# Six h buffers in a pool of their own, spread transfers and later turns in a fused attention and gated-unit kernel

## The chip, the cores and the metric

The kernel runs on one core of a Trainium2 chip. The core's engines work side by side and meet only at semaphores: TensorE (PE in the profile, its weight loads PEld), VectorE (DVE), ScalarE (ACT), GpSimd (POOL) and SyncE (SP), which here only issues transfers. The metric is the device time of one execution in microseconds (us), the median of several runs; lower is better. A profiled execution is one more run, with its own time.

## The reference

All of it is float32, with 2048 positions, 640 channels and 1536 hidden units.

```python
xn = layernorm(x)                                  # x: (1, 2048, 640)
q, k, v = split(xn @ wqkv)                         # 32 heads of 20 channels
idx = pos[:, None] - 2 * arange(8)[None, :]        # each position sees itself and 7 earlier ones, 2 apart
logits = where(idx >= 0, q . k[idx] * 20 ** -0.5, -1e9)
o = softmax(logits) . v[idx]
s = o @ wo
h = (xn @ w_gate) * (xn @ w_up)                    # no nonlinearity between
out = x + s * silu(h @ w_down)
```

## The kernel before

**Arithmetic.** A matmul of full precision is made of three: each operand is split into a high part (ScalarE copies it to the matmul's type, L109 and others) and a low part (the difference, on GpSimd or VectorE, L110 and others), and high x high, high x low and low x high are added up in one PSUM bank. The profile shows 4054 such matmuls. Gate and up, the output projection and the down projection also use seven products in place of eight for a two by two block (`group`, `pair_product`, `product`), which costs sums of operands on VectorE and GpSimd and adds of results.

**Stages, in TensorE's order.** (1) To about 45 us x is loaded, normalised and transposed into xT, four chunks of 512 columns, each with a high and a low part. (2) To about 274 us the queries, keys and values are made, unit by unit: a unit is a group of 4 or 6 heads (GROUPS) at even or odd positions (r), 12 in all. ScalarE copies each result to a staging buffer (L441), and every second tile is sent to memory, qkv_scr (L445). Between these, gate and up are made for the first hidden blocks. (3) To about 525 us gate and up of the other blocks: `group(f, c0, second)` makes hidden block f for two chunks. (4) The output projection, in pairs of tiles (`pair_product`, L1033, p from 0 to 4) and then single tiles. (5) From about 600 us the down projection, the gate and the result.

**Attention** runs beside stages 2 and 3 on VectorE and GpSimd. It is a generator, `attention()`: `advance(budget)`, called after each piece of TensorE work, lets it emit as many of its steps as the budget pays for. This fixes the program order; nothing is reordered later, and each engine works its instructions off in order. For unit n a round goes over j = 0, 2, 4, 6: two keys' products (L527), one term of the values of unit n-1 (L498, its addition on GpSimd, L504), the reduction to logits (L534), another term of the values. After the round come the store of unit n-1's result (`store_o`, L575) and the softmax. `ahead(n, parts)` issues the loads of a unit on SP's queue: part 0 is `load_kq` (queries L408, keys L414 and L416), part 1 the values (the same lines, in the other half of the kv buffer). It does so once for each unit and part, and only when the unit is in qkv_scr. There are two kv buffers and one q buffer; ScalarE copies the queries on to PSUM (L488).

**The buffers of h.** Tag "gh" holds 128x512 tiles in 5 buffers. Each group takes four: `hold(j)` copies a partial product out of PSUM (L1295) for j = 0, 2, 1 and 4 of its order 0, 5, 2, 1, 4, 3, 6. Three banks A, C and B carry the seven products, so the next product into a bank waits until the hold before it has read that bank. The sums of a group are gate_b (L1298), up_b (L1301), gate_a (L1308), up_a (L1311) and h_b (L1304); up_a and h_b go to `unfinished` and are emitted by `finish_piece` after the first product of the next group. `store_h` (L1284) sends the two results to h_scr, and only then are two of the buffers free.

**SP's queue** carries loads and stores in program order; an instruction that waits holds up all those behind it. Before the change `group` issues the weights of the next block (`load_wf`, L175, two buffers "wraw") ahead of its first product, so they stand before the two h stores of the group before. GpSimd makes sums of weights (L1272, `w_add`) and low parts (L110, `w_split`).

**Early sums.** `early_sums(0)` is a generator of eight GpSimd steps (L593). EARLY of them are emitted ahead of `scales(8)`, three more behind it, the rest behind `scales(12)`. `spread(8)` multiplies the scales (L340) amid `gate_up(0, 1)`.

**The end of stage 3.** `beside` holds what is emitted after a named product: (f0, 1, 4) is `sums_wo` (L936 to L939), (f0, 1, 5) and (f0, 1, 6) the splits of wo's blocks 0 and 1 on VectorE, (f1, 0, 0) `turn_pair(0)` and `load_pair(1)`, where f0 = 10 and f1 = 11 are the last hidden blocks. `turn_pair(p)` is two transposes (L710) and four differences (L982 to L985) on VectorE; `hi_pair` (L1008, ScalarE) and `lo_pair` (L1012, VectorE) split its parts; `pair_product` adds up results at L1039, L1042 and L1044.

Of the kernel before, what the change touches and what calls it, by code (L numbers as in the profile page):

```python
# [43 lines left out]
PAIRS = range(0, W, 2)  # L44
PACE = 1.0
VEC = 3
EARLY = 3
GROUP_RATE = 0.184


# [6 lines left out]
def kernel(  # L57
# [15 lines left out]

    sb = ctx.enter_context(tc.tile_pool(name="sb", bufs=1))
    ps = ctx.enter_context(tc.tile_pool(name="ps", bufs=2, space=PSUM))
    dr = ctx.enter_context(tc.tile_pool(name="dr", bufs=1, space=DRAM))
    ctx.enter_context(tc.manual_schedule())

# [1 line left out]

    def st(shape, tag, bufs, dt=F32):
        cnt[0] += 1
        return sb.tile(shape, dt, tag=tag, bufs=bufs, name=f"{tag}_{cnt[0]}")

    ring, turns = [], [0]

# [333 lines left out]
    def qkv(m, r, i, runs=ALL_RUNS, at=None, act=None, bank=("q", 3)):  # L420

        c = MC[m]
        p = pt([P, 3 * c], *bank)
        t0 = (i % TPC) * P
        for n, (a, b, k) in enumerate(runs):
            if n == at:
                act()
            nc.tensor.matmul(p, xT[(r * NE + i) // TPC][a][:, k, t0:t0 + P], wq[m][b][k], start=n == 0,  # L428
                             stop=n == len(runs) - 1, skip_group_check=act is not None)
        if m or r:  # L430
            if not staged:
                y = slot([P, 2, 2 * 3 * CMAX], F32)
                staged.extend([y[:, 0], y[:, 1], st([P, 2 * 3 * CMAX], "pk", 1)])
            if c > CMAX and not wide:
                wide.extend([slot([P, 6 * c], F32), st([P, 6 * c], "pk", 1)])
            if i % 2 == 0:
                now[0] = wide if c > CMAX else staged
                now[0].insert(0, now[0].pop())
            n = len(MADE[m])
            y = now[0][0][:, :6 * c].rearrange("p (n a i c) -> p n a i c", n=n, a=3, i=2)  # L440
            nc.scalar.activation(y[:, :, :, i % 2, :].rearrange("p n a c -> p a n c"),  # L441
                                 p.rearrange("p (a n c) -> p a n c", a=3, n=n), AF.Copy)
            for k, g in enumerate(MADE[m]):
                if i % 2:
                    nc.scalar.dma_start(scr[2 * g + r][:, :, i - 1:i + 1, :], y[:, k])  # L445
                if i == NE - 1:
                    made.add(2 * g + r)
            if c > CMAX and (r, i) == (DIL - 1, NE - 1):
                staged.clear()
            return  # L450
        u = 0
        nc.scalar.activation(kv_t[u][:, :, W - 1 + i, :], p[:, c:].rearrange("p (a c) -> p a c", a=2), AF.Copy)
        nc.scalar.activation(q_t[u][:, i, :], p[:, :c], AF.Copy)
        for i0, i1 in ((1, 5), (5, NE)):
            if i == i1 - 1:
                for p0, p1 in ((0, 112), (112, 127)):
                    nc.sync.dma_start(kv_t[u][p0 + 1:p1 + 1, :, i0 - 1:i1 - 1, :],
                                      kv_t[u][p0:p1, :, W - 1 + i0:W - 1 + i1, :])


    def attention():
# [45 lines left out]
        for n, u in enumerate(ORDER + [None]):  # L507
            if u is not None:
                late_unit = u not in made
                while u not in made:  # L510
                    yield None
                ahead(n, (0, 1))
                for _ in range(5 if late_unit else 0):
                    yield None
                g, r = UN[u]
                nh = GROUPS[g]
                c = nh * DH
                copy_q(n)
                q, kv = q_two[:, :NE * c].unsqueeze(1).to_broadcast([P, 2, NE * c]), kv_t[u]
                lg = st([P, NE * nh, W], "lg", 2)  # L520
                t = twice.rearrange("p a c -> p (a c)")[:, :2 * NE * c].rearrange("p (a c) -> p a c", a=2)
            for j in PAIRS:
                if u is not None:
                    ahead(n + 1, (0,))
                    k = flat(kv[:, 0, j:j + NE, :])
                    k = bass.AP(k.tensor, k.offset, [k.ap[0], [c, 2], k.ap[1]])
                    nc.vector.tensor_mul(t, q, k)  # L527
                    yield 2 * NE * c * 1.22e-3
                if before is not None:
                    cost, add = values(j)  # L530
                    add()
                    yield cost
                if u is not None:
                    nc.vector.tensor_reduce(out=lg[:, :, j:j + 2].rearrange("p n a -> p a n"),  # L534
                                            in_=t.rearrange("p a (n d) -> p a n d", d=DH), op=ALU.add, axis=AX.X)
                    yield 2 * NE * c * 1.2e-3
                if before is not None:
                    cost, add = values(j + 1)
                    add()
                    yield cost  # L540
            if u is None:
                store_o(before)
                ring[:] = three
                return
            ahead(n + 1, (0, 1))
            if before is not None:
                store_o(before)
            m0 = lg[0:1].rearrange("p (i h) w -> p i h w", h=nh)
# [688 lines left out]
    def two(f):  # L1237
        return F_TWO <= f < f1
# [48 lines left out]
    def group(f, c0=0, second=0):  # L1287
# [26 lines left out]
        if not second:  # L1314
            if not two(f - 1):
                w_split(f, "U")
            w_sum.pop(f, None)
            wf_raw.pop(f)
            if f < f1 and f + 1 not in wf_raw:
                load_wf(f + 1)  # L1320
        for n, j in enumerate((0, 5, 2, 1, 4, 3, 6)):
            y = b["ACACABA"[j]]
            runs = [(w_unit(f, H_IN[j], k)[i], x_in(W_IN[j], l, k, c0)) for i, l in ALL3 for k in range(2)]
# [15 lines left out]
                places[second, n](f)  # L1339
            if (f, second, n) in beside:  # L1340
                beside[f, second, n]()
            advance(PACE * len(runs) * (GROUP_RATE if two(f) else 0.184))

    places = {}
# [54 lines left out]
    for m, t in ((m, t) for m in range(1, len(MADE)) for t in range(DIL)):  # L1399
# [23 lines left out]
        elif (m, r) == (last, 1):  # L1423
            for k in range(2):
# [3 lines left out]
    w_sum.pop(2)  # L1428
    load_wf(3)
    beside.update({(f0, 0, 5): lambda: advance(1e9), (f0, 1, 0): lambda: begin_last(), (f0, 1, 1): lambda: load_pair(0),  # L1430
                   (f0, 1, 4): lambda: sums_wo(), (f0, 1, 5): lambda: split_wo(0, nc.vector),
                   (f0, 1, 6): lambda: split_wo(1, nc.vector)})

    def begin_last():
        advance(1e9)
# [19 lines left out]
    for f in range(2, f1):  # L1455
# [18 lines left out]
        if f == F_TWO:  # L1474
# [1 line left out]
        group(f, 2)  # L1476
        group(f, 0, 1)
    places.clear()
    beside.update({(f1, 0, 0): lambda: (turn_pair(0), load_pair(1)), (f1, 0, 4): lambda: (hi_pair(0, 0), lo_pair(0, 0)),
                   (f1, 0, 6): lambda: (hi_pair(0, 1), lo_pair(0, 1), load_e(3, 1, 3)), (f1, 0, 5): sum_w5,  # L1480
                   (f1, 0, 3): lambda: load_e(3, 0, 2)})
    group(f1)
# [19 lines left out]
    split_wo(3)  # L1502
    split_w5()
    g3 = gate(f1, 3)
    turn_pair(2)
    up(f1, 3, g3)
    finish_piece()
    begin_wd()
    begin_wd("B22")
    pair_k.append(st([P, 3, HALF], "o", 1))  # L1510
    wd_steps = [(k, part) for k in range(KH) for part in range(2)]

    to_split = []
# [18 lines left out]
    for p in range(SP // 2):  # L1532
# [32 lines left out]
        pair_product(p, 5)  # L1565
        if p == 0:
            load_pair(4)
        elif p == 1:
            turn_pair(3)
        elif p == 2:  # L1570
            load_o(SP, 3, st([P, 3, D], "t", 2))
            turn_pair(4)
        else:
            if p == 3:
                load_o(SP + 3, 3, st([P, 3, D], "t", 2))
            wd_sums()
# [98 lines left out]
```

## Time and profile before

| | us |
|---|---|
| median of 3 runs | 748.58 (748.15 to 749.75) |
| the profiled execution, its own time | 748.28 |
| its span, first to last instruction | 746.5 |
| granted TensorE clock in it | 1.000 |
| ScalarE busy | 302.5 |
| GpSimd busy | 462.6 |
| transfers, mean | 178 GB/s |

A row of waits gives the engine with its tile and line, what released it, and then us in total, times, and the longest in us. A row of the timeline gives start and length in us, engine, line, operation, out<-in, sizes, how many instructions are merged, and in brackets how long the engine sat idle before and what ended that. A row of stretches gives from:to, length, then busy us of PE, PEld, DVE, ACT and POOL with the number of instructions, the granted clock, the transfers' share and GB/s. A row of the page's groups gives line, engine, operation, out<-in, sizes and count, then busy us and mean ns of one, then idle us before them and what ended most of it. A row of transfers gives tiles, issuing engine, count, KB each, and the median us from issue to landing. Lines such as L896 are line numbers of the kernel.

### The profile page before, as it was taken

The numbers are of one execution on the slowest core, as the hardware profiler recorded it, in microseconds if no ns is written. First come the engines' busy times: TensorE is split into PE (matmuls) and PEld (weight loads), VectorE is DVE, ScalarE is ACT, GpSimd is POOL, SyncE is SP. The second block draws the span as 40 slices with busy tenths as digits, with TensorE's granted clock in tenths as the row PEclk, the third lists the DMA queues.
The fourth block names the chain that finished last, engine by engine and source line by source line (L and its number), as shares of the span: only waits on it lengthen the run. The fifth ranks groups of instructions, "written<-read, shape, count | busy, mean of one in ns | idle before, by whom it ended". The sixth has DMA issues, their size and how long they took to land. (4 is left out here: it accounts for less than half of the span.)

```text
span 746.5 us, 11102 instructions
## 1 busy us (share of the span) xinstructions
PE 735.4 (99%) x4054; PEld 669.0 (90%) x4054; DVE 612.2 (82%) x720; ACT 302.5 (41%) x577; POOL 462.6 (62%) x389
## 2 busy tenths in 40 slices
PE   8999999999999999999999999999999999999997
PEld 6989989988999998778887888887899999999997
DVE  7666998699697887998999999667998777777775
ACT  5658413323332332233223322335556564444442
POOL 6169929787688878888879989877559800000000
PEclk9999999999999999999999999999999999999999
DMA  9465672947446548856165424268567655555534
GB/s 316 170 202 200 236 224 87 299 157 239 127 152 197 190 128 232 274 161 207 55 159 149 115 82 110 72 178 204 167 177 212 228 220 191 191 191 191 191 106 141
DMA packets 103493, 132.98 MB, mean 178 GB/s; under 512 B 22696, under 2 KB 74404, under 8 KB 103438
## 3 DMA queue, kind: packets, MB, share of 16 engines
q1 hardware_dynamic: 84686, 112.77, 48.4%
q10 hardware_dynamic: 17600, 14.26, 5.9%
q0 software_dynamic: 1152, 5.24, 2.2%
q8 instruction: 32, 0.52, 0.3%
q14 instruction: 23, 0.19, 0.1%
HBM read 83.58 MB, written 47.81 MB: 176 GB/s over the span
## 5 line engine op out<-in xcount | busy, mean ns | idle before, releaser
L504 POOL TENSOR_TENSOR o<-o,t 128x960 f32<-128x960 f32 (+1 forms) x69 | 139.6, 2024 | 19.1 <-DVE t L498 17.6
L498 DVE TENSOR_TENSOR t<-e,kv 128x960 f32<-128x960 f32 (+1 forms) x96 | 99.4, 1037 | 24.8 <-POOL o L504 24.7
L527 DVE TENSOR_TENSOR t<-q,kv 128x1920 f32<-128x1920 f32 (+1 forms) x48 | 92.4, 1925 | 4.3 <-DMA kv<-qkv_scr 4.2
L534 DVE TENSOR_REDUCE lg<-t 128x96 f32<-128x1920 f32 (+1 forms) x48 | 92.3, 1922 | 0.2
L428 PE MATMUL q<-s,xc 128*128 128x360 f32 (+1 forms) x450 | 83.1, 334 | 0.6 <-DVE lg L266 0.5
L110 POOL TENSOR_TENSOR s<-wraw,s 128x384 fp32r<-128x384 f32 (+6 forms) x58 | 69.6, 1210 | 19.9 <-ACT s L109 19.9
L428 PEld LDWEIGHTS q<-s,xc 128*128 128x128 f32 x450 | 74.9, 188 | 4.8 <-DVE lg L266 0.8
L1295 ACT ACTIVATE gh<-g 128x512 f32<-128x512 f32 x54 | 32.2, 597 | 115.8 <-PE g L1328 97.8
L428 PE MATMUL u<-s,xc 128*128 128x360 f32 (+1 forms) x360 | 65.8, 334 | 0.0
L428 PEld LDWEIGHTS u<-s,xc 128*128 128x128 f32 x360 | 60.3, 188 | 2.3
L428 PE MATMUL g<-s,xc 128*128 128x360 f32 (+1 forms) x330 | 61.5, 337 | 0.0
L428 PEld LDWEIGHTS g<-s,xc 128*128 128x128 f32 x330 | 55.7, 188 | 2.6
L1328 PE MATMUL u<-xc,s 128*128 128x512 f32 x216 | 55.3, 391 | 0.9 <-ACT gh L1295 0.9
L896 PE MATMUL q<-xc,s 128*128 128x320 f32 x342 | 55.5, 309 | 0.0
L1328 PE MATMUL g<-s,s 128*128 128x512 f32 x216 | 55.0, 390 | 0.0
L896 PEld LDWEIGHTS q<-xc,s 128*128 128x128 f32 x342 | 51.5, 188 | 0.0
L1328 PEld LDWEIGHTS u<-xc,s 128*128 128x128 f32 x216 | 40.3, 188 | 10.5 <-ACT gh L1295 2.0
L1328 PEld LDWEIGHTS g<-s,s 128*128 128x128 f32 x216 | 40.5, 188 | 8.6 <-ACT gh L1295 0.2
L109 ACT ACTIVATE s<-wraw 128x384 fp32r<-128x384 f32 (+6 forms) x59 | 33.5, 587 | 29.5 <-PE g L1328 9.0
L504 POOL TENSOR_TENSOR o<-t 128x960 f32<-128x960 f32 (+1 forms) x12 | 24.4, 2032 | 31.8 <-DVE t L498 25.2
L1328 PE MATMUL g<-xc,s 128*128 128x512 f32 x168 | 41.5, 391 | 1.3 <-ACT gh L1295 1.3
L119 PE MATMUL g<-xc,s 128*128 128x512 f32 (+1 forms) x180 | 40.1, 373 | 0.0
(367 smaller groups left out, 1566.5 us busy)
## 6 DMA issues: line engine op xcount, KB each, us to landing
h_scr<-gh SPq DMA_DIRECT2D x48, 256.0 KB, 2.6
wraw<-in_wgu SPq DMA_DIRECT2D x11, 640.0 KB, 4.4
kv<-qkv_scr SPq DMA_DIRECT2D x14, 480.0 KB, 5.9
qkv_scr<-s ACTq DMA_DIRECT2D x18, 360.0 KB, 4.4
t<-h_scr SPq DMA_DIRECT2D x8, 768.0 KB, 7.1
kv<-qkv_scr SPq DMA_DIRECT2D x14, 367.5 KB, 6.6
s_scr<-gh SPq DMA_DIRECT2D x16, 320.0 KB, 4.2
gh<-s_scr SPq DMA_DIRECT2D x16, 320.0 KB, 3.5
```

The costliest lines, as they stand in the source:

```text
L109: nc.scalar.activation(hi, raw, AF.Copy)
L110: eng.tensor_sub(lo, raw, hi.bitcast(F32))
L119: nc.tensor.matmul(acc, a, b, start=first and n == 0, stop=last and n == len(runs) - 1)
L428: nc.tensor.matmul(p, xT[(r * NE + i) // TPC][a][:, k, t0:t0 + P], wq[m][b][k], start=n == 0, stop=n == len(runs) - 1, skip_group_check=ac ...
L498: nc.vector.tensor_mul(t.rearrange("p (n d) -> p n d", d=DH), e[:, :, w].unsqueeze(2).to_broadcast([P, NE * nh, DH]), v)
L504: return NE * c * cost, lambda: eng.tensor_add(y, z, t)
L527: nc.vector.tensor_mul(t, q, k)
L534: nc.vector.tensor_reduce(out=lg[:, :, j:j + 2].rearrange("p n a -> p a n"), in_=t.rearrange("p a (n d) -> p a n d", d=DH), op=ALU.add, ax ...
L896: nc.tensor.matmul(p, y[:, i, k], wd_t[name][k][:, l], start=new and r == 0, stop=r == len(runs) - 1, skip_group_check=True)
L1295: nc.scalar.activation(kept[j], b["ACACABA"[j]], AF.Copy)
L1328: nc.tensor.matmul(y, w, x, start=j in (0, 1, 5) and r == 0, stop=r == len(runs) - 1, skip_group_check=True)
```

## The change

Six things, all in the order or the place of work; no matmul is added or removed.

- EARLY is 1 instead of 3.
- The tag "gh" moves out of the common pool into one of its own with 6 buffers, up to the last gate and up product. Then that pool is closed and one with 5 buffers takes its place.
- The four stores of staged results of unit 1 (m = 0, r = 1) are issued by SP instead of ScalarE.
- In attention the loads are spread: the values of unit n are asked for at j = 2 of its round (before: at the end of the round of n-1), the keys and queries of unit n+1 from j = 4 on (before: from j = 0 on). A unit that was made late still loads both at once.
- `group` issues the weights of the next block after its first product, so behind `finish_piece` and the two h stores.
- The splits of wo's blocks 0 and 1 each move by one product, `turn_pair(0)` and `load_pair(1)` by two, and `turn_pair(2)` from before the last up product to the end of pair 0, behind its sums and `load_pair(4)`.

```diff
-EARLY = 3
+EARLY = 1
...
+    halfway = ExitStack()
+    gh_pool = [halfway.enter_context(tc.tile_pool(name="six", bufs=1)), 6]
...
-        return sb.tile(shape, dt, tag=tag, bufs=bufs, name=f"{tag}_{cnt[0]}")
+        pool = sb
+        if tag == "gh":
+            pool, bufs = gh_pool
+        return pool.tile(shape, dt, tag=tag, bufs=bufs, name=f"{tag}_{cnt[0]}")
...
-                    nc.scalar.dma_start(scr[2 * g + r][:, :, i - 1:i + 1, :], y[:, k])
+                    (nc.scalar if m else nc.sync).dma_start(scr[2 * g + r][:, :, i - 1:i + 1, :], y[:, k])
...
-                ahead(n, (0, 1))
+                ahead(n, (0, 1) if late_unit else (0,))
...
-                    ahead(n + 1, (0,))
+                    if j == 2:
+                        ahead(n, (1,))
+                    elif j > 2:
+                        ahead(n + 1, (0,))
...
-            ahead(n + 1, (0, 1))
+            ahead(n + 1, (0,))
...
-            if f < f1 and f + 1 not in wf_raw:
-                load_wf(f + 1)
...
             if (f, second, n) in beside:
                 beside[f, second, n]()
+            if (second, n) == (0, 0) and f < f1 and f + 1 not in wf_raw:
+                load_wf(f + 1)
...
-                   (f0, 1, 4): lambda: sums_wo(), (f0, 1, 5): lambda: split_wo(0, nc.vector),
-                   (f0, 1, 6): lambda: split_wo(1, nc.vector)})
+                   (f0, 1, 4): lambda: sums_wo(), (f0, 1, 6): lambda: split_wo(0, nc.vector)})
...
-    beside.update({(f1, 0, 0): lambda: (turn_pair(0), load_pair(1)), (f1, 0, 4): lambda: (hi_pair(0, 0), lo_pair(0, 0)),
+    beside.update({(f1, 0, 0): lambda: split_wo(1, nc.vector),
+                   (f1, 0, 2): lambda: (turn_pair(0), load_pair(1)), (f1, 0, 4): lambda: (hi_pair(0, 0), lo_pair(0, 0)),
...
     g3 = gate(f1, 3)
-    turn_pair(2)
     up(f1, 3, g3)
...
     pair_k.append(st([P, 3, HALF], "o", 1))
+    halfway.close()
+    gh_pool[:] = [ctx.enter_context(tc.tile_pool(name="five", bufs=1)), 5]
...
         if p == 0:
             load_pair(4)
+            turn_pair(2)
```

## The prediction

> **What bounds the kernel now.** I read the page's shares first, then who TensorE waits for, then the stretches in which it waits.
>
> ```profile
> span 746.5 us, 11102 instructions
> ...
> PE 735.4 (99%) x4054; PEld 669.0 (90%) x4054; DVE 612.2 (82%) x720; ACT 302.5 (41%) x577; POOL 462.6 (62%) x389
> ```
>
> TensorE is busy 99% of the span and the change leaves its 4054 products alone, so it can win only what TensorE loses in waits. The waits of the matmuls, and below them those of the weight loads (us in total, times, longest):
>
> ```profile
> PE g L1328 <- ACT gh L1295: 1.3, 2, 0.9
> PE e L340 <- POOL lg L334: 1.0, 1, 1.0
> PE u L1328 <- ACT gh L1295: 0.9, 2, 0.6
> PE e L1033 <- DVE xc L1012: 0.8, 1, 0.8
> ...
> PEld g L1328 <- ACT gh L1295: 2.6, 4, 1.3
> PEld u L1328 <- ACT gh L1295: 2.0, 3, 1.0
> PEld e L340 <- POOL lg L334: 1.4, 1, 1.4
> ...
> PEld e L1033 <- DVE xc L1012: 1.0, 1, 1.0
> ...
> PEld g L1328 <- POOL pk L110: 0.5, 1, 0.5
> ```
>
> Three places carry nearly all of it: the gate and up products, which wait for ScalarE's copies into h buffers (L1295); the spread of the scales (L340), which waits for GpSimd; and the first output products (L1033), which wait for a low part on VectorE. (The last row, a wait for a split of weights, is touched by no edit.) A matmul's end is modelled, so its wait is the low bound of a loss; the weight load that stands before it waits longer and is the high bound. Low: 1.3 + 0.9 + 1.0 + 0.8 = 4.0 us. High: 2.6 + 2.0 + 1.4 + 1.0 = 7.0 us. More than 7.0 us isn't there to be won, while work moved to a worse place can cost more than that. How full the other engines are (busy us of PE, PEld, DVE, ACT, POOL in a stretch):
>
> ```profile
> 60.00:300.00 240.00, 240.00 (x1319) 223.75 (x1318) 198.74 (x182) 81.96 (x159) 190.87 (x139) 1.00 0.62 193
> 300.00:490.00 190.00, 188.27 (x824) 153.95 (x823) 174.17 (x170) 58.41 (x98) 161.85 (x122) 1.00 0.46 134
> ...
> 540.00:550.00 10.00, 10.00 (x70) 10.00 (x69) 9.81 (x18) 6.48 (x15) 5.51 (x5) 1.00 0.63 193
> ```
>
> Up to 300 us VectorE has 240 - 198.74 = 41 us to spare and GpSimd 49; beside the gate and up products 15.8 and 28.2; in the output products VectorE has 0.2 us in ten. These limits decide how much of a removed wait is kept.
>
> **EARLY from 3 to 1.** Two of GpSimd's early sums move behind scales(8).
>
> ```profile
> 43.79 2.55 POOL L593 TENSOR_TENSOR kv<-xc 128x512 f32<-128x512 f32 x2 [17.92 <-DVE xc L370]
> ...
> 45.02 0.17 DVE L277 RECIPROCAL lg<-lg 128x4 f32<-128x4 f32 x1
> ...
> 47.55 0.21 POOL L278 TENSOR_TENSOR lg<-lg 128x4 f32<-128x4 f32 x1
> ...
> 49.46 0.41 PE L340 MATMUL e<-lg,lg 128*128 128x32 f32 x2 [1.03 <-POOL lg L334]
> ```
>
> One sum (2.55 us for two) ends at 45.07, and the reciprocal that L278 needs ends at 45.19, so the scales start at 45.2 instead of 47.55. From there to the product it took 49.46 - 47.55 = 1.9 us: ready at 47.1, and TensorE asks at 49.46 - 1.03 = 48.4. The wait goes with 1.3 us to spare: 1.0 to 1.4, taken 1.2. The two sums come back behind scales(12), so GpSimd's early work ends about as much later as one of them lasts, 1.3 us; the 49 us that it has up to 300 hide that.
>
> **Stores of the first unit on SP's queue.** Four issues leave ScalarE. TensorE has no wait for L441's copies in the list, so nothing is won. On SP the last two stand behind the stores of early_high(1) and the copies into e_scr, and unit 1's keys are asked for behind them, so VectorE may start unit 1 later; its 41 us hide that, and without them the price is one wait for keys (4.2 us on VectorE, the row for L527 below). Taken 0 for TensorE, 0 to 4.2 if the cover is gone.
>
> **Six h buffers, and transfers spread.** What a copy into h waits for:
>
> ```profile
> 391.27 0.93 SPq L1284 DMA_DIRECT2D h_scr<-gh  x2
> ...
> 398.25 0.60 ACT L1295 ACTIVATE gh<-g 128x512 f32<-128x512 f32 x1 [2.98 <-DMA h_scr<-gh]
> ...
> 398.90 2.34 PE L1328 MATMUL g<-xc,s 128*128 128x512 f32 x9 [0.87 <-ACT gh L1295]
> ...
> 507.36 0.60 ACT L1295 ACTIVATE gh<-u 128x512 f32<-128x512 f32 x1 [2.63 <-POOL gh L1304]
> ```
>
> ```profile
> h_scr<-gh SPq DMA_DIRECT2D x48, 256.0 KB, 2.6
> ...
> kv<-qkv_scr SPq DMA_DIRECT2D x14, 480.0 KB, 5.9
> ```
>
> The two stores were out by 392.2, but the buffer came free only at 398.25, six us on, where the median store lands in 2.6: the next unit's queries and keys had been asked for just ahead of them. A group claims four buffers in 54 matmuls; at 2.34 / 9 = 0.26 us each that is 14 us, so a sixth buffer puts off each claim by up to 3.5 us. Of waits of 2.98 and 2.63 nothing is left then. Near 507 it helps further that both early splits of wo now stand behind the gate's sum on VectorE. The rows above give 2.2 to 4.6; taken 3.4. Where the five buffers follow the six, the first claim (L1039) may wait until the last h store has landed, 2.6 us at most, once; VectorE is ahead there by the move of turn_pair(2), so 0 is taken.
>
> The key loads that are asked for half a round later cost nothing by themselves:
>
> ```profile
> L527 DVE TENSOR_TENSOR t<-q,kv 128x1920 f32<-128x1920 f32 (+1 forms) x48 | 92.4, 1925 | 4.3 <-DMA kv<-qkv_scr 4.2
> ```
>
> After j = 4 two such products of 1.9 us are left, two reductions over the same elements, and the value products and softmax between them: 7.7 us and more, against 5.9 for a transfer. Without that cover VectorE waits, as it did once, for 4.2 us. Values have a whole round.
>
> The load of the next weights (load_wf) now stands behind both stores of the group before, and the second of them waits for GpSimd's L1304:
>
> ```profile
> 379.77 3.39 SPq L1284 DMA_DIRECT2D h_scr<-gh  x2
> ...
> 384.92 0.77 POOL L1272 TENSOR_TENSOR wraw<-wraw 128x256 f32<-128x256 f32 x1
> ...
> 421.63 1.57 POOL L110 TENSOR_TENSOR pk<-wraw,pk 128x640 fp32r<-128x640 f32 x1
> ...
> 425.65 1.52 PE L1328 MATMUL g<-xc,pk 128*128 128x512 f32 x6
> ```
>
> ```profile
> wraw<-in_wgu SPq DMA_DIRECT2D x11, 640.0 KB, 4.4
> ```
>
> In the tightest of seven groups it goes out at 379.77 + 3.39 = 383.2 and lands at 387.6, while the first sum over it began at 384.92: GpSimd waits 2.7 us, inside its 28.2. What matters more: weights for a next group were split by 423.20 and used at 425.65, 2.45 us on. With 1.2 + 3.4 = 4.6 us won, TensorE would come 2.1 us before them unless GpSimd and VectorE move up too, for which they have idle time in part. Given back: 0 to 2.1, taken 1.1.
>
> **Pairs turned later.** turn_pair(0) and the four transfers of load_pair(1) move by two products of a group; the wait of 3.79 us here takes that, since pair 0 is wanted only at 525.8:
>
> ```profile
> 519.33 0.69 DVE L1370 TENSOR_TENSOR gh<-g,gh 128x512 f32<-128x512 f32 x1 [3.79 <-PE g L119]
> ...
> 523.41 1.67 DVE L983 TENSOR_TENSOR t<-t,s 128x256 f32<-128x256 f32 x1
> ...
> 525.83 0.45 PE L1033 MATMUL q<-s,kv 128*128 128x320 f32 x2
> ```
>
> Pair 2 moves behind the sums of pair 0:
>
> ```profile
> 527.73 1.56 DVE L710 STREAM_TRANSPOSE s<-s 128x640 f32<-128x640 f32 x2
> ...
> 529.78 0.42 DVE L983 TENSOR_TENSOR s<-s,s 128x256 f32<-128x256 f32 x1
> ...
> 532.41 1.50 DVE L1012 TENSOR_TENSOR xc<-s,xc 128x640 fp32r<-128x640 f32 x1
> ...
> 533.96 0.56 PE L1033 MATMUL e<-s,xc 128*128 128x320 f32 x2 [0.78 <-DVE xc L1012]
> ...
> 541.13 0.48 DVE L1042 TENSOR_TENSOR gh<-o,e 128x320 f32<-128x320 f32 x1
> ...
> 543.12 1.04 PE L1033 MATMUL e<-xc,xc 128*128 128x320 f32 x6
> ```
>
> turn_pair(2) is 1.56 + 4 x 0.42 = 3.2 us, and the low part at 532.41 stands behind it. Without it that part is ready 3.2 us earlier and the wait is gone: 0.8 to 1.0, taken 0.9. The 3.2 us then fall before pair 1's sums. There L1042 ends at 541.61, and the product that overwrites its bank begins at 543.12: 1.5 us of room. The rest must fit into the time that VectorE no longer spends on it before. Given back: 0 to 3.2, taken 0.3, near the low end because the piece only changes places on an engine that was the late one here. Next late is L1042 in pairs 1 to 3.
>
> Four such differences took 1.67 us each beside GpSimd's splits (523.41) and 0.42 away from them (529.78). The Trainium skill (SBUF — State Buffer, Who interferes with whom) says that a VectorE tensor_tensor with both inputs in SBUF and a GpSimd instruction that reads SBUF shut each other out for a whole instruction; the trace agrees, 1.67 against 0.42, and by that rule the new place, next to the splits of wd, is the worse one. What such a place makes of the sum is rival 4.
>
> **Sum**, against the profiled execution's 748.28 us (0.3 below the median of the runs, 748.58): 748.28 - 1.2 - 3.4 - 0.9 + 1.1 + 0.3 = 744.2 us.
>
> **Rivals.** (1) Everything is kept, at the high bound: 748.28 - 7.0 = 741.3. For it: 15.8 and 28.2 us of idle time beside the groups; against: only 2.45 us of room before the weights. (2) Attention's two engines set the pace: the copies no longer wait, but the split weights come as late as before, and of the 3.4 us nothing is kept: 748.28 - 1.2 - 0.9 + 0.3 = 746.5. For it: VectorE is busy 174.17 of 190 us there. Against: only 0.5 us of weight loads waited for such a split. (3) The change doesn't do what it says: the copies wait for late work, not for a place, and new waits replace the old: about 748. (4) VectorE becomes the bound of the output products. It has 0.2 us in ten there, so turn_pair(2) is paid in full, and beside the splits of wd with 4 x (1.67 - 0.42) = 5.0 us more, 8.2 in all, handed on by each pair's sums: 748.28 - 5.5 + 1.1 + 8.2 = 752.1. It outweighs the rest from 4.4 us of lateness up. Against: the row at 529.78 and the 1.5 us of room at 541.61.
>
> **How the numbers follow.** Forecast 0.55; its own range goes from 748.28 - 7.0 with half of the 1.4 given back, 742.0, to 748.28 - 4.0 + 2.1 = 746.4. (1) 0.09; (2) 0.10; (3) 0.08; (4) 0.18. About 0.2%, 1.5 us, is what a measurement of this kernel can tell from no change. Faster are the forecast, (1) and (2): 0.74; same is (3): 0.08; slower is (4): 0.18. From 741.0 to 748.7 the range leaves out (4) and little else.
>
> **What would show it.** Right: no wait of L340 for L334; copies of L1295 that wait for TensorE, no more for h_scr or L1304; no wait of L1033 for L1012 near 533, and turn_pair(2) near 535 with differences of about 0.42. Wrong: weight loads of L1328 waiting for L110 between 300 and 490 (case 2), L1272 waiting for in_wgu by more than 3 us in a group, or L1033 waiting for L1042 in pairs 1 to 3 (case 4).

## The result, and the profile after

| | before | changed |
|---|---|---|
| median of 5 runs each, us | 748.95 (748.15 to 750.33) | 744.86 (744.34 to 745.49) |
| ratio to before, 95% interval | | 0.9942 [0.9928, 0.9957] |
| the profiled execution, us | 748.28 | 744.50 |
| its span, us | 746.5 | 742.7 |

The kernel became faster by 4 us; 744.2 had been forecast. From here lines are those of the kernel that is spoken of; in the changed one L345 is the spread (L340 before), L1303 the copies into h (L1295), L1292 the h stores (L1284), L1041 the pairs' products (L1033), L1020 the low parts (L1012), and L1047, L1050 and L1052 the pairs' sums (L1039, L1042, L1044).

The changed kernel's page, first its span and the engines' busy time:

```profile
span 742.7 us, 11094 instructions
...
PE 734.2 (99%) x4054; PEld 669.7 (90%) x4054; DVE 612.5 (82%) x720; ACT 301.9 (41%) x577; POOL 463.5 (62%) x389
```

The work is the same on every engine within 1.2 us; what has changed is the waits. Who the matmuls wait for in the changed kernel (us in total, times, longest):

```profile
PE q L1041 <- DVE gh L1050: 1.4, 1, 1.4
...
PE e L1041 <- ACT o L1044: 0.4, 1, 0.4
PE e L1041 <- DVE gh L1050: 0.4, 1, 0.4
PE g L1334 <- ACT gh L1303: 0.2, 1, 0.2
```

The spread's wait and the low part's are gone, the copies' waits are down from 2.2 to 0.2 us, and a new wait of 1.4 us stands in the pairs. What that comes to is read from the starts of matmuls, since nothing else is between them. The list of a line's matmuls gives first and last starts; the differences between four of them cut the execution into stages (us):

| stage | ends at | length before | changed | difference |
|---|---|---|---|---|
| 1 | last product of the spread, L340 / L345 | 56.7 | 54.9 | -1.8 |
| 2 | first product of the groups, L1328 / L1334 | 217.2 | 217.2 | 0.0 |
| 3, groups | first product of the pairs, L1033 / L1041 | 251.9 | 248.1 | -3.8 |
| 4, pairs | last product of the pairs | 43.5 | 45.7 | +2.1 |
| 5 | last matmul | 172.1 | 172.1 | -0.1 |

Together -3.6 of the 3.8 us between the two executions. Of stage 1, 0.5 us is there already at the first product of the spread (28.98 and 28.50), ahead of any edit; the same moment lies between 28.5 and 29.2 in the kernels below, whatever they change. That leaves 1.3 us for the spread. So the groups gave more than was forecast, and the pairs, where a gain had been forecast, lost 2.1 us.

The stretches of the changed kernel that answer to two shown before (from:to, length, busy PE, PEld, DVE, ACT, POOL):

```profile
300.00:490.00 190.00, 189.79 (x837) 156.83 (x837) 171.73 (x169) 60.21 (x101) 163.77 (x125) 1.00 0.47 141
...
540.00:550.00 10.00, 9.88 (x68) 9.62 (x67) 9.74 (x18) 6.07 (x15) 4.50 (x4) 1.00 0.53 169
```

In the groups TensorE is now busy 189.79 of 190 us instead of 188.27. In the pairs VectorE is as full as it was, 9.74 of 10.

### The profile page after: what moved, and what is told of

Same layout as the page of the kernel before. It is cut to its first block, busy times and chain, and to the rows that moved or that the text cites. A ratio compares the mean times of both kernels' runs of the same rounds, so it can differ in the third digit from the quotient of the medians.

```text
span 742.7 us, 11094 instructions
## 1 busy us (share of the span) xinstructions
PE 734.2 (99%) x4054; PEld 669.7 (90%) x4054; DVE 612.5 (82%) x720; ACT 301.9 (41%) x577; POOL 463.5 (62%) x389
## 5 line engine op out<-in xcount | busy, mean ns | idle before, releaser
L433 PE MATMUL q<-s,xc 128*128 128x360 f32 (+1 forms) x450 | 83.0, 334 | 0.0
L115 POOL TENSOR_TENSOR s<-wraw,s 128x384 fp32r<-128x384 f32 (+6 forms) x58 | 69.9, 1215 | 20.0 <-ACT s L114 18.5
L433 PEld LDWEIGHTS q<-s,xc 128*128 128x128 f32 x450 | 75.0, 188 | 4.1 <-POOL s L115 0.4
L1303 ACT ACTIVATE gh<-g 128x512 f32<-128x512 f32 x54 | 32.3, 598 | 109.9 <-PE g L1334 108.9
L433 PE MATMUL u<-s,xc 128*128 128x360 f32 (+1 forms) x360 | 65.7, 334 | 0.0
L433 PEld LDWEIGHTS u<-s,xc 128*128 128x128 f32 x360 | 60.2, 188 | 2.3
L433 PE MATMUL g<-s,xc 128*128 128x360 f32 (+1 forms) x330 | 61.5, 337 | 0.0
L433 PEld LDWEIGHTS g<-s,xc 128*128 128x128 f32 x330 | 55.7, 188 | 2.6
L1334 PE MATMUL g<-s,s 128*128 128x512 f32 x216 | 54.8, 389 | 0.0
L1334 PE MATMUL u<-xc,s 128*128 128x512 f32 x216 | 54.8, 389 | 0.0
L1334 PEld LDWEIGHTS u<-xc,s 128*128 128x128 f32 x216 | 40.5, 188 | 8.5
L1334 PEld LDWEIGHTS g<-s,s 128*128 128x128 f32 x216 | 40.5, 188 | 8.4
L1334 PE MATMUL g<-xc,s 128*128 128x512 f32 x168 | 41.3, 390 | 0.2 <-ACT gh L1303 0.2
```

The source lines that it names most:

```text
L115: eng.tensor_sub(lo, raw, hi.bitcast(F32))
L1303: nc.scalar.activation(kept[j], b["ACACABA"[j]], AF.Copy)
L1334: nc.tensor.matmul(y, w, x, start=j in (0, 1, 5) and r == 0, stop=r == len(runs) - 1, skip_group_check=True)
```

## The experiments

Each kernel was run beside the kernel before on the same chip, in three series; before's medians there were 749.59 (17 runs), 749.47 (23) and 749.72 (24). "Six alone", "early alone", "turn alone" and "early and stores" are the kernel before with one part of the change; the others are the changed kernel with one part undone or altered. "Changed, first" is the result above, with its own runs of before. Stages are those of the table above, from each kernel's own profiled execution, in us:

| kernel | median | ratio, 95% interval | stage 1 | 2 | 3 | 4 |
|---|---|---|---|---|---|---|
| before | | | 56.7 | 217.2 | 251.9 | 43.5 |
| turn alone | 749.34 | 0.9999 [0.9988, 1.0009] | 56.5 | 217.2 | 252.9 | 43.5 |
| early alone | 751.17 | 1.0028 [1.0017, 1.0039] | 55.2 | 218.9 | 254.1 | 43.6 |
| early and stores | 748.83 | 0.9990 [0.9976, 1.0004] | 55.3 | 217.2 | 252.6 | 43.6 |
| six alone | 747.76 | 0.9978 [0.9968, 0.9988] | 56.6 | 217.2 | 250.1 | 44.5 |
| changed, first | 744.86 | 0.9942 [0.9928, 0.9957] | 54.9 | 217.2 | 248.1 | 45.7 |
| changed, again | 745.63 | 0.9952 [0.9935, 0.9969] | 55.6 | 219.5 | 247.8 | 45.7 |
| five | 745.55 | 0.9951 [0.9938, 0.9965] | 55.4 | 217.2 | 249.9 | 44.7 |
| five, loads back | 749.04 | 0.9994 [0.9984, 1.0004] | 55.1 | 217.2 | 253.1 | 44.7 |
| weights back | 745.48 | 0.9959 [0.9943, 0.9974] | 54.9 | 217.2 | 248.7 | 45.8 |
| turn back | 745.34 | 0.9946 [0.9926, 0.9965] | 55.0 | 220.2 | 248.4 | 44.5 |
| last h elsewhere | 744.64 | 0.9939 [0.9921, 0.9957] | 55.0 | 217.2 | 248.8 | 43.9 |
| last h elsewhere, turn back | 745.40 | 0.9949 [0.9931, 0.9967] | 55.4 | 217.2 | 249.1 | 44.5 |
| last h elsewhere, sums on GpSimd | 743.06 | 0.9921 [0.9905, 0.9938] | 54.9 | 217.2 | 248.2 | 43.4 |

How far a stage repeats is seen where its code is the same: stage 3 lies between 247.8 and 248.8 in the four kernels that have all of the change's groups (two "changed", "last h elsewhere", and the last row), and differs by 1.0 between "before" and "turn alone", whose edit comes only at the end of that stage; there the matmuls wait 3.6 us for copies into h against 2.2 in "before". Stage 4 repeats better: 45.7, 45.7 and 45.8 in the three with the changed pairs.

### The new wait in the pairs

In the changed kernel, timelines of SP, VectorE and TensorE around the first pair (start, length, engine, line):

```profile
524.92 0.38 SPq L1292 DMA_DIRECT2D h_scr<-gh  x1
...
525.16 0.81 DVE L1020 TENSOR_TENSOR xc<-s,xc 128x640 fp32r<-128x640 f32 x1
528.29 0.49 DVE L1047 TENSOR_TENSOR gh<-o,u 128x320 f32<-128x320 f32 x1 [2.31 <-DMA h_scr<-gh]
528.69 0.48 DVE L1050 TENSOR_TENSOR gh<-o,q 128x320 f32<-128x320 f32 x1
...
529.23 1.14 PE L1041 MATMUL q<-xc,kv 128*128 128x320 f32 x6 [1.36 <-DVE gh L1050]
...
538.13 1.14 PE L1041 MATMUL e<-xc,xc 128*128 128x320 f32 x6 [0.37 <-DVE gh L1050]
```

L1047 writes the first tile of the pool with five buffers, which lies where the pool with six lay. It waits until the last h has been stored: issued at 524.92, free at 528.29. VectorE stands still for 2.31 us, the sum behind it, L1050, reads its bank late, and the product that overwrites that bank waits 1.36 us. If the place is the cause, the wait must go when the last h lies elsewhere; if the lateness comes from turn_pair(2) or from VectorE's load, it stays.

**Last h elsewhere.** The last h lies in a tile that isn't of tag "gh":

```diff
-            hs = st([P, CH], "gh", 5)
+            hs = st([P, CH], "gh", 5) if (f, ch) != (f1, NCH - 1) else slot([P, CH], F32)
```

> The changed kernel, with one tile moved: the last product of gate and up (block 11, chunk 3) is written to a slot of tag s and not to an h buffer. Theory A (hand-over: the first of the five buffers waits until the last h store out of the six has landed): the wait of the first pair sum (L1047) for h_scr, 2.3 us in the changed kernel's profile, goes, and with it TensorE's 1.4 us for L1050; 744.9 becomes 742.8 to 743.6. Theory B (the turn of pair 2 in its new place makes VectorE the bound of the pairs): VectorE is late anyway, TensorE still waits over 1 us for the sums of pairs 0 and 1, and the time stays within 744.4 to 745.4.

VectorE's timeline of that kernel, and below it the waits of its matmuls:

```profile
526.00 0.81 DVE L1020 TENSOR_TENSOR xc<-s,xc 128x640 fp32r<-128x640 f32 x1
526.74 0.47 DVE L1047 TENSOR_TENSOR gh<-o,u 128x320 f32<-128x320 f32 x1
527.14 0.48 DVE L1050 TENSOR_TENSOR gh<-o,q 128x320 f32<-128x320 f32 x1
```

```profile
PE e L1041 <- ACT o L1044: 0.4, 1, 0.4
PE e L1041 <- DVE gh L1050: 0.4, 1, 0.4
```

The sum follows the low part without a gap, TensorE's 1.4 us are gone, and the pairs take 43.9 instead of 45.7. So the place is the cause, and it cost 1.7 us of TensorE's time. The whole execution shows less of it: 744.64 against 744.86, with intervals that overlap, and not the 742.8 to 743.6 of theory A. In the profiled execution stage 3 came out 0.7 longer, within its scatter. What is left is another thing: VectorE has no gap from 526 to 558 there. The starts of the products, counted from the first one and set against those of the kernel before, fall back by 0.6, 0.4 and 0.4 us where products wait for sums in pairs 1 to 3, and by 0.6 at a wait for ScalarE's copy (L1044) in pair 4.

**Turn back**, with turn_pair(2) in its old place:

```diff
     g3 = gate(f1, 3)
+    turn_pair(2)
...
             load_pair(4)
-            turn_pair(2)
```

> The changed kernel with turn_pair(2) back in its old place, before the last up product. Theory A (hand-over): the 3.2 us of the turn cover the landing of the last h store, so no wait for h_scr is left, but the low part behind the turn is late as before the change; TensorE loses 1 to 2 us around the first pair instead of 1.8, and the time is 744.3 to 745.3, the move being worth nothing by itself here. Theory B (the new place is the worse one): 2 us or more are won back and the time is 742.5 to 743.3.

Its matmuls' waits:

```profile
PE e L1041 <- DVE xc L1020: 1.7, 1, 1.7
```

The hand-over's wait is hidden: VectorE works on turn_pair(2) while the h store lands. In its place the low part is late, as before the change, but by 1.7 us where it was 0.8. Two things make it later: VectorE begins the turn 2.3 us after the first product of the pairs (1.9 before), and three of the four differences take 0.77 to 1.12 us instead of 0.42; what stands behind them is shorter and gives back a part. The pairs take 44.5, and the time, 745.34, is at the upper edge of theory A's range.

**Both**, the last h elsewhere and turn_pair(2) back:

> Both edits together: the last product of gate and up in a slot of tag s, and turn_pair(2) in its old place. Theory A: nothing waits for the hand-over in either, so the turn alone decides, and its old place costs about the 0.8 to 1.9 us that TensorE lost there before the change: 743.8 to 745.0, slower than the kernel with only the last product moved by 0.5 to 1.9 us. Theory B: faster than that kernel.

The same 1.7 us for the low part and the same 44.5 us. Beside "last h elsewhere" this gives the worth of the turn's new place where no hand-over disturbs it: 44.45 - 43.95 = 0.5 us in the pairs, and 0.8 by the medians, though their intervals overlap and 745.40 lies a little above the 745.0 that had been expected.

**Turn alone**, in the kernel before:

```diff
     g3 = gate(f1, 3)
-    turn_pair(2)
...
             load_pair(4)
+            turn_pair(2)
```

> The kernel before with only turn_pair(2) moved behind pair 0's sums. There is no hand-over here, five buffers throughout. Theory A: the wait of the output products for the low part (0.8 to 1.0 us) goes and little comes back: 748.95 becomes 747.5 to 748.5. Theory B: VectorE is the bound, waits for the sums of pairs 1 to 3 appear, and the time is 749.0 to 751.0.

Nothing: ratio 0.9999 [0.9988, 1.0009], and 43.5 us for the pairs with it and without. The matmuls no longer wait for L1012, and after pair 0 the products are 1.9 us ahead of the kernel before, counted from the first product of the pairs. Then they lose 0.4 us at a wait for L1042 in each of pairs 1 to 3 and 0.6 at a wait for ScalarE's copy in pair 4, and at the last product 0.1 us is left. So the waits of theory B came. In the stretches of this kernel around pair 1 VectorE is nearly full:

```profile
520.00:540.00 20.00, 20.00 (x122) 18.83 (x122) 19.26 (x24) 10.27 (x22) 13.73 (x10) 1.00 0.69 188
540.00:550.00 10.00, 9.89 (x67) 9.63 (x67) 9.81 (x17) 5.87 (x14) 6.22 (x6) 1.00 0.49 163
```

Here, moving a piece on an engine that is nearly full changed which products wait, and not what they lose together.

**Sums on GpSimd.** If VectorE is what bounds the pairs, taking work off it must help. Besides the last h elsewhere, the sums of wd (L797 to L809 before) of the first two blocks go to GpSimd:

```diff
     def sum_wd(k, part, half):
         r = wd_raw[k]
+        eng = nc.gpsimd if k < 2 else nc.vector
...
-            nc.vector.tensor_sub(v["T1"], r[:, 0, 1], r[:, 0, 0])
+            eng.tensor_sub(v["T1"], r[:, 0, 1], r[:, 0, 0])
```

(the three other sums likewise)

> The changed kernel with the last product of gate and up in a slot of tag s, and with the sums of wd for its first two blocks (four subtractions for each block) on GpSimd instead of VectorE. Theory A (in the pairs VectorE is the bound, busy without a gap from 520 to 558 us in the kernel with only the slot): 4 us of 128x320 sums less... eight of 0.48 us, 3.9 us in all over four pairs, so the four waits of 0.3 to 0.5 us for the sums of pairs 1 to 3 go and the time is 1 to 1.8 us below the changed kernel's. Rival (GpSimd's sums shut VectorE out for as long as they save): the waits stay within 0.3 us of what they were and the time is that of the kernel with only the slot, 0 to 0.9 us below the changed kernel.

The same stretch with the last h elsewhere, and then with the sums on GpSimd as well:

```profile
520.00:540.00 20.00, 19.63 (x130) 18.91 (x129) 19.83 (x27) 10.89 (x24) 14.86 (x11) 1.00 0.48 136
```

```profile
520.00:540.00 20.00, 19.76 (x134) 19.42 (x133) 17.99 (x24) 12.03 (x26) 17.69 (x16) 1.00 0.48 125
```

VectorE's share falls from 19.83 to 17.99 us, GpSimd takes it up, and the pairs take 43.4, the least of all. The waits for the sums did not go, as theory A had it: 0.3 and 0.2 us stand in the list of matmuls where 0.4 stood. Half of the 0.6 us is won by the end of pair 0, the rest by pair 3. By its median, 743.06, this is the fastest kernel here, 0.9921 [0.9905, 0.9938] of before. Against the changed kernel the pairs give 45.7 - 43.4 = 2.3 us: 1.7 by the last h and 0.6 by the sums; the medians of the same series say 2.6 (745.63), more than either theory gave. The gain comes although the differences of turn_pair(3) now lie beside GpSimd's sums, at 0.99 us each:

```profile
539.91 0.99 DVE L992 TENSOR_TENSOR t<-t,s 128x256 f32<-128x256 f32 x1
```

### Buffers or transfers

In the groups three edits act together: the sixth buffer, the spread loads, and the weights behind the stores.

**Six alone**, the kernel before with the pools of six and then five:

```diff
+    halfway = ExitStack()
+    gh_pool = [halfway.enter_context(tc.tile_pool(name="six", bufs=1)), 6]
...
+    halfway.close()
+    gh_pool[:] = [ctx.enter_context(tc.tile_pool(name="five", bufs=1)), 5]
```

> The kernel before with only the h buffers changed: six in a pool of their own, then five. Theory A (the copies waited for a place): TensorE's waits for L1295 go nearly whole, 2.2 to 4.6 us of weight loads, and the hand-over gives some back; 748.95 becomes 745.3 to 747.3. Rival (the copies waited for late work and for the order on SP's queue): waits for the copies stay at over half, and the time is above 747.5.

Its matmuls' waits:

```profile
PE e L1038 <- DVE xc L1017: 1.7, 1, 1.7
...
PE u L1333 <- POOL s L115: 1.1, 1, 1.1
...
PE g L1333 <- ACT gh L1300: 0.3, 1, 0.3
```

The copies' waits are down to 0.3 us, but a split of weights on GpSimd (L115) is now late by 1.1, and the low part of the pairs by 1.7. The groups gain 251.9 - 250.1 = 1.8 us, the pairs give 0.9 back; the whole is 0.9978 [0.9968, 0.9988], 1.7 us (1.1 between the profiled executions). By the waits for copies theory A holds. The gain over the same series' 749.47 lies at the low edge of what it gave, 1.7 to 3.7 us, as the two new waits take part of it.

**Five**, the changed kernel with five buffers in one pool to the end:

```diff
-    gh_pool = [halfway.enter_context(tc.tile_pool(name="six", bufs=1)), 6]
+    gh_pool = [halfway.enter_context(tc.tile_pool(name="six", bufs=1)), 5]
...
-    halfway.close()
-    gh_pool[:] = [ctx.enter_context(tc.tile_pool(name="five", bufs=1)), 5]
```

(and halfway = ctx)

> The changed kernel with five h buffers from beginning to end, in one pool. Theory (the sixth buffer does the work): waits of TensorE for the copies come back, 1 to 4 us, while the hand-over's 1.4 us go; 745.0 to 748.0. Rival (the order on SP's queue does it, stores ahead of the weights and loads spread): the waits for copies stay under 0.5 us and, without the hand-over, the time is 743.0 to 744.0.

Neither came whole. TensorE's matmuls wait only 0.4 us for the copies, as the rival had it, but the time, 745.55, is the theory's, with groups of 249.9. The weight loads wait 1.7 us for copies, and 0.6 with six buffers. Without a hand-over the pairs take 44.7, 0.8 more than in "last h elsewhere": a copy on ScalarE (L1044) is late by 0.7 us there. Why is open.

**Five, loads back**: as five, but queries, keys and values asked for as in the kernel before, three lines of attention():

```diff
-                ahead(n, (0, 1) if late_unit else (0,))
+                ahead(n, (0, 1))
...
-                    if j == 2:
-                        ahead(n, (1,))
-                    elif j > 2:
-                        ahead(n + 1, (0,))
+                    ahead(n + 1, (0,))
...
-            ahead(n + 1, (0,))
+            ahead(n + 1, (0, 1))
```

> The changed kernel with five h buffers from beginning to end and attention's loads as before the change, so that of the transfers only the next block's weights stand behind the h stores. Theory (the order of keys and values ahead of h stores made the copies late): with five buffers waits for L1295 come back to 1.5 us or more, and the time is 0.5 to 2.5 us above the kernel with five buffers and spread loads (745.55). Rival (the place of the weights is what mattered): the waits stay near 0.4 us and the time within 0.4 us of 745.55.

The two kernels with five buffers differ by 3.5 us in the median and by 253.1 - 249.9 = 3.2 in the groups, a little more than the theory gave. With the loads back the matmuls wait 2.7 us for the copies, as it had it, against 0.4. SP's timeline and ScalarE's show how, first with the loads as before:

```profile
384.92 4.21 SPq L413 DMA_DIRECT2D q<-qkv_scr  x1
389.17 0.43 SPq L419 DMA_DIRECT2D kv<-qkv_scr  x1
389.65 0.92 SPq L421 DMA_DIRECT2D kv<-qkv_scr  x2
390.66 0.93 SPq L1289 DMA_DIRECT2D h_scr<-gh  x2
...
396.60 0.60 ACT L1300 ACTIVATE gh<-g 128x512 f32<-128x512 f32 x1 [3.67 <-DMA h_scr<-gh]
```

and with the loads spread:

```profile
387.24 0.96 SPq L1292 DMA_DIRECT2D h_scr<-gh  x2
388.25 0.53 SPq L419 DMA_DIRECT2D kv<-qkv_scr  x1
...
392.91 0.60 ACT L1303 ACTIVATE gh<-g 128x512 f32<-128x512 f32 x1 [0.76 <-PE g L1334]
```

In the first, the h stores stand on SP's queue behind four loads, one of which takes 4.21 us to get away, and are then under way together with those loads: the copy waits for them until 396.60. In the second they go out ahead of the loads. The lists of transfers between 380 and 400 us give the median from issue to landing of an h store, first with the loads as before, then spread:

```profile
h_scr<-gh SPq DMA_DIRECT2D x3, 256.0 KB, 5.9
```

```profile
h_scr<-gh SPq DMA_DIRECT2D x3, 256.0 KB, 2.3
```

So the order alone brings the copies' waits down with five buffers; whether the stores are slow because they start behind the loads or because they share the way with them isn't told apart. The sixth buffer adds 249.9 - 248.1 = 1.8 us in the groups, about as much as alone, each with a scatter of up to 1 us; in the whole time the hand-over takes that back (745.55 against 744.86 and 745.63). The change with six buffers and the loads as before was not run; from "six alone" to "changed" the groups gain another 2.0, which holds all edits but the buffers.

**Weights back**, the changed kernel with load_wf ahead of the group's first product:

```diff
             wf_raw.pop(f)
+            if f < f1 and f + 1 not in wf_raw:
+                load_wf(f + 1)
...
-            if (second, n) == (0, 0) and f < f1 and f + 1 not in wf_raw:
-                load_wf(f + 1)
```

> The changed kernel with the next block's weights asked for ahead of the group's first product again, so ahead of the h stores. Theory (six buffers leave room for late stores): no wait for the copies comes back, GpSimd no longer waits for in_wgu (7.5 us in six places in the changed kernel), and the time is unchanged, 744.4 to 745.4. Rival (the order on SP's queue matters): stores are late again, waits for copies of 0.5 us or more, 745.5 to 747.

SP's waits between 300 and 490 us in that kernel, and TensorE's in the groups:

```profile
SPq L180 <- POOL s L115: 55.9, 7, 11.7
```

```profile
PE g L1336 <- ACT gh L1303: 0.3, 1, 0.3
```

SP stands before a load of weights for 55.9 us in seven pieces, with the h stores behind it, and TensorE loses nothing by it: 248.7 us for the groups, within their scatter. GpSimd waits for in_wgu only once, 2.0 us, against 7.5 in six places, as the theory had it. With six buffers the place of the weights can't be told from no edit.

### The early sums and the first unit's stores

**Early alone**, the kernel before with EARLY = 1:

```diff
-EARLY = 3
+EARLY = 1
```

> The kernel before with only EARLY = 1. Theory: the wait of the spread (1.0 to 1.4 us) goes and all of it reaches the end, 747.5 to 748.0. Rival (later stages are bound by attention's engines, which do not move up): the wait goes, but waits for h buffers or for split weights grow by as much behind it, and the time stays at 748.5 to 749.3.

Slower: 1.0028 [1.0017, 1.0039], outside both ranges. Stage 1 is shorter, as it should be, but stage 2 is longer by 1.7 us and stage 3 by 2.2; the matmuls' waits for copies into h grow from 2.2 to 5.1 us, of the kind that the rival named. ScalarE's and TensorE's timelines near 88 us:

```profile
88.27 0.54 ACTq L445 DMA_DIRECT2D qkv_scr<-s  x1
88.91 0.47 ACT L441 ACTIVATE pk<-g 128x360 f32<-128x360 f32 x1 [8.19 <-DMA t_scr<-t]
...
89.79 2.58 PE L119 MATMUL u<-xc,s 128*128 128x512 f32 x10 [1.38 <-ACT pk L441]
```

The kernel before at the same place:

```profile
85.38 0.52 ACTq L445 DMA_DIRECT2D qkv_scr<-s  x1
86.00 0.47 ACT L441 ACTIVATE pk<-g 128x360 f32<-128x360 f32 x1 [3.82 <-DMA t_scr<-t]
```

A store that ScalarE is to issue waits for another store, t_scr, that SP issued. In the kernel before this holds ScalarE for 3.8 us and nobody waits for it; with the early sums moved it holds it for 8.2, and TensorE waits 1.4 for the copy that frees its bank.

**Early and stores**: EARLY = 1, and the stores of unit 1 on SP.

```diff
-                    nc.scalar.dma_start(scr[2 * g + r][:, :, i - 1:i + 1, :], y[:, k])
+                    (nc.scalar if m else nc.sync).dma_start(scr[2 * g + r][:, :, i - 1:i + 1, :], y[:, k])
```

> The kernel before with EARLY = 1 and the first unit's four stores on SP. Alone, EARLY = 1 made ScalarE wait 8.2 us behind such a store and TensorE 1.4 us near 88 us. Theory (the two belong together: the store on ScalarE's queue is what takes EARLY's gain back): the wait near 88 is gone, that of the spread too, and the time is 2 to 3.5 us below EARLY alone, at -1.5 to 0 us against the kernel before. Rival (EARLY's gain is lost in the gate and up stage whatever the stores do): the wait near 88 goes, but the waits for L1295 grow to 4 us and more, and the time is not below the kernel before.

ScalarE's timeline there:

```profile
85.14 0.47 ACT L441 ACTIVATE pk<-u 128x360 f32<-128x360 f32 x1 [1.93 <-PE u L428]
```

It waits for TensorE alone again, and stage 2 is back at 217.2. Over the whole, the two edits together give 0.9990 [0.9976, 1.0004]: 2.3 us less than EARLY alone by the medians, and against the kernel before no difference that the interval can tell, though stage 1 is 1.4 us shorter. That is what the theory gave; the waits for L1295 are 2.0 us, so the rival's did not come. Both kernels have longer groups than before (254.1 and 252.6 against 251.9), the first by more than the scatter; why is open.

### The changed kernel again

> The changed kernel once more, beside the other three on one chip. Nothing is edited: 744.3 to 745.7, with the hand-over wait of the first pair sum (2.3 us) and TensorE's 1.4 us behind it.

The waits in the groups and pairs are those of the first profile, and yet this execution took 747.3 us. All of the difference lies in stage 2, 219.5 against 217.2, where the products of L433 are slower by a little each. Its costliest row, in the first profile and then in the second (busy us, mean ns):

```profile
L433 PE MATMUL q<-s,xc 128*128 128x360 f32 x375 | 65.9, 326 | 0.0
```

```profile
L433 PE MATMUL q<-s,xc 128*128 128x360 f32 x375 | 66.6, 327 | 0.7 <-DVE lg L271 0.7
```

The rows of the same line and size into u and g have 0.8 and 0.6 us more (48.7 and 49.5, 41.0 and 41.6), which makes 2.1 with this one. Nearly all of it arises from about 200 us on: 158 products lie between 205 and 230 us in the first profile and 154 in the second. "Turn back" shows the same from there on; of its 220.2, another 0.8 us is a wait for a ScalarE copy. The cause is open; it is why the experiments are compared by stages and not only by their times.

## Why the prediction was right, and where it wasn't

The time came within 0.7 us of the forecast, but that is in part luck, since two errors of opposite sign met: the groups gave 1.5 us more and the pairs 2.7 us less than the sum said.

**The bound and the places.** Right. The three waits named were those that could be won, and the spread and the groups gave 1.3 + 3.8 = 5.1 us, where their part of the bounds is 3.2 to 6.0 (4.0 and 7.0 less the 0.8 and 1.0 of the output products). The third wait went too, but most of its gain was lost again.

**EARLY.** Right in size, 1.3 against 1.2. Timelines of GpSimd and TensorE in the changed kernel:

```profile
43.32 1.29 POOL L601 TENSOR_TENSOR kv<-xc 128x512 f32<-128x512 f32 x1 [18.13 <-DVE xc L375]
44.80 0.20 POOL L283 TENSOR_TENSOR lg<-lg 128x4 f32<-128x4 f32 x1 [0.18 <-DVE lg L282]
...
46.60 1.30 POOL L601 TENSOR_TENSOR kv<-xc 128x512 f32<-128x512 f32 x1
...
47.79 0.30 PE L345 MATMUL e<-lg,lg 128*128 128x32 f32 x2
```

One sum, then the scales at 44.80, and the product goes at 47.79 without a wait.

**The stores of unit 1.** "TensorE has no wait for L441's copies in the list, so nothing is won" failed. It asked what the wait on ScalarE cost before, and not what it costs once EARLY has moved the work around it. "Early alone" shows the cover used up: 1.7 us in stage 2, which the stores' move takes back. The two edits are one; the sum is unharmed only because both were made. The Trainium skill (DMA: Bandwidth & Descriptors, Issuing engines are not separate DMA queues) says that issuing on several engines saves only the sequencer's time of issuing, usually small beside the transfer. The issue itself took 0.54 us here; what the move saved beside "early alone" was ScalarE's 8.2 us of standing before it.

**The groups.** The 3.4 us were right in kind, and the 1.1 given back did not come. The split weights are late by 1.1 us in "six alone", where rival (2) shows itself; in the changed kernel no matmul of the groups waits for L115 (in "last h elsewhere" and "last h elsewhere, turn back" one does, by 0.2 and 0.3 us), and between 300 and 490 us this is the only row of the weight loads' waits:

```profile
PEld g L1334 <- ACT gh L1303: 0.6, 1, 0.6
```

So the other edits took nearly all of that wait away. Which of them was not told apart, though "weights back" doesn't bring it again. Within the 3.8 us the sixth buffer is worth 1.8, while the loads' order is worth 3.2 where there are five: that stores in time do as much as a further buffer had been seen in the row of 398.25, but the sum gave one figure for both.

**What was costed at nothing.** Right: products of keys still wait 4.1 us for a load, once (4.3 before), and GpSimd waits for a load of weights by 2.6 us at most, where 2.7 had been worked out. From the changed kernel's groups and GpSimd's waits:

```profile
L535 DVE TENSOR_TENSOR t<-q,kv 128x1920 f32<-128x1920 f32 (+1 forms) x48 | 92.5, 1927 | 4.1 <-DMA kv<-qkv_scr 4.0
```

```profile
POOL wraw L1280 <- DMA wraw<-in_wgu: 7.5, 6, 2.6
```

**The hand-over.** This is the step that failed: "VectorE is ahead there by the move of turn_pair(2), so 0 is taken", with 2.6 us as the bound. Being ahead is what makes it wait: with turn_pair(2) in front, VectorE comes when the store has landed; without it, 2.31 us too soon. A cover was taken away by the same edit that was given as the reason for its being enough. Cost: 1.7 us in the pairs.

**turn_pair(2).** -0.9 and +0.3 were summed to a gain of 0.6. Alone it gains 0.0, and beside the other edits 0.5, once the hand-over is out of the way. Both terms were too small: in "turn alone" 1.9 us are won by the end of pair 0 and 1.8 given back, where 0.3 had been taken. The "1.5 us of room" was read at one product; what decides is that VectorE has 0.2 us in ten. The remaining 0.4 us of the pairs' loss (43.9 against 43.5) is 0.9 - 0.5: in "last h elsewhere, turn back" the low part is late by 1.7 us where it was 0.8, and the pairs take 0.9 longer than before. TensorE reaches the pairs 4.1 us earlier there, VectorE begins the turn only 3.7 us earlier (524.05 against 527.73), and its differences take longer, as in "turn back".

**Rival (4)** was right in what bounds the pairs and wrong in the price. Its sign came: a product of pair 1 waits 0.37 us for L1050 at 538.13. The price was read too high at its source, since the four differences of turn_pair(0) took 1.85, 1.67, 1.67 and 1.10 us and not 1.67 each. The differences at the new place took what they take away from GpSimd's work, and not 1.67:

```profile
533.15 0.42 DVE L991 TENSOR_TENSOR s<-s,s 128x256 f32<-128x256 f32 x1
```

The rule of the Trainium skill (SBUF — State Buffer, Who interferes with whom) isn't contradicted by this, since GpSimd had no work at that moment. In the kernel with sums on GpSimd it had, and the differences took 0.99; the exchange paid all the same.

## What to carry to other kernels

When tiles of a new pool take the place of an old one, find the last reader of the old one, a store above all, and what the first writer of the new one does until then; an edit that brings this writer forward uncovers the wait. Where an engine is full in a stage, moving work within it gained 0.0 and 0.5 us here, and moving some of it to another engine gained 0.6 more, even at a worse price each. Stores that free a buffer belong ahead of loads that nobody needs yet: their order was worth 3.2 us of the groups here, with five buffers, and one more buffer 1.8.

## What had not been expected of the hardware

- A store on ScalarE's queue stood 3.8 us, and 8.2 after an edit elsewhere, until a store of another tensor from SP's queue had landed, and ScalarE's copies stood behind it. What ties the two isn't to be seen in the trace.
- A 256 KB store landed in 2.3 us ahead of the loads and in 5.9 us behind them, on one queue.
- The same kernel took 217.2 and 219.5 us for its second stage in two executions, at a granted clock of 0.999 in both, by products that were up to 1.6% slower (48.7 and 49.5 us for one row of L433), nearly all of it after 200 us.
